# Block-sparse attention feeding a GELU MLP on one Trainium2 core: sampled value rows fetched by GpSimd row gathers from an SBUF list instead of block copies from registers

## The chip, the cores and the metric

One core of a Trainium2 chip runs the whole program: TensorE (PE; its weight loads are listed as PEld), VectorE (DVE), ScalarE (ACT), GpSimd (POOL) and SyncE (SP), each with its own in-order instruction queue, and 16 DMA engines that serve the DMAs which SP, POOL and ACT issue. The metric is the device time of one execution, in microseconds.

## The reference

Batch 4, 8 heads, 768 tokens, head size 64, all in float32. Tokens are in 24 blocks of 32. A query block sees itself and its neighbours, the first and the last block, and three sampled blocks; the first and the last query block see everything. The result goes, token by token, through a two-layer network.

```python
mask = np.abs(blk_i - blk_j) <= window            # window = 1
mask = mask | (blk_i == 0) | (blk_j == 0) | (blk_i == n_blocks - 1) | (blk_j == n_blocks - 1)
for qb in range(n_blocks):
    for kb in sampled_blocks[qb]:                 # 3 random blocks, int64
        mask[qb * block:(qb + 1) * block, kb * block:(kb + 1) * block] = True
scores = np.where(mask, scores, -1e9)             # scores = q k^T / 8, softmax, times v
...
x = attn_out.transpose(0, 2, 1, 3).reshape(B * S, H * D)     # 3072 x 512
h = x @ w_in                                      # 512 -> 2048
g = 0.5 * h * (1.0 + erf(h * inv_sqrt2))
return g @ w_out                                  # 2048 -> 512
```

A sampled block may repeat another one, or lie in the window or among the global blocks; it counts once.

## The kernel before

The work is cut into eight units, (batch b, half hf) for b = 0..3 and hf = 0, 1; a unit is 12 query blocks (384 tokens). For each unit the kernel runs attention and then the first layer (`ffn1_step`, 8 steps, PE then GELU on ACT); the second layer (`ffn2_pieces`) is fed as filler between the steps of the *next* unit's attention. The order on every engine is the order of the Python program (the schedule is manual), and the framework adds the semaphore waits.

A unit has 8 groups: two for its dense block (4 heads each) and six of one or two sparse blocks. For a sparse block all eight heads' scores stand in two rows of 256 columns: 96 of the window, 96 sampled, 32 + 32 of the two global blocks. `stage_scores` (L309) makes them on PE, DVE takes the maximum (L329), `stage_exp` (L347) the exponential on ACT, `stage_transpose` and `stage_evict` (L359, L367) turn the probabilities, `stage_av` (L388) multiplies them with the values, `stage_x` brings the result into `xT` for the first layer.

Gathered operands lie in SBUF. `kg` holds, for the 11 sparse blocks of a unit, the sampled keys (columns 0 to 95) and the global keys (96 to 159); it is filled by copies out of `kT` at an offset in a register (`k_sampled`, L251; `k_unit` shares them out between POOL and DVE) and by `k_globals` (L242). There is one `kg` for all units. The window's keys are read straight from `kT`. Values go a longer way: v is loaded (`load_v`: two halves of heads `vx` and the rows of the first and last block, `vgl`), copied on DVE or ACT into `vn` (`v_rows`, with columns of ones for the sum), written to a scratch in DRAM (`v_scratch`, `vscr`, one row of 528 numbers = 1056 bytes per token, and a 25th block of zeros), and read back as the operands `vg0s`, `vg1s` (one pair per half, 128 rows each): window rows by `v_window` (L282), sampled blocks by `v_sampled` (L265), one DMA of 32 rows (33 KB) for each of 11 x 3 sampled blocks of a unit, global rows by copies from `vgl` (`v_ends`, L272 to L277). A sampled block that repeats another or lies in the window reads the block of zeros instead; `value_list` (L173) works out these numbers once on DVE, 5 us of short operations on 72 numbers. Block numbers used as offsets are loaded into registers of the engine that issues (`block_numbers`, L205).

Row order in the value operands before: `vg0s` rows 0 to 95 window, 96 to 127 sampled 0; `vg1s` rows 0 to 63 sampled 1 and 2, 64 to 127 global. The columns of the scores are in the same order.

What sets the order around the change: POOL's queue carries all loads of inputs and weights (they cast to bf16), half of the key copies, the `v_ends` of the first halves, and 108 of the 264 sampled value DMAs; SP's queue carries the scratch writes, the window DMAs, 156 sampled value DMAs and the output stores. At the start POOL issues k, q, `vgl`, k, q, v; then `v_ends(0, 0)`, 18 key copies for blocks 6 to 11, then values mixed with the weight loads. PE starts with 36 transposes of the identity (L524) that nobody reads, then transposes k and q (`prep_pair`, L224). During the first layer of unit (0,0) the lists for the second half are loaded and `second_values` (L556) issues the second half's values and then the loads of batch 1. From unit 1 on, `steps` holds what is issued between the first layer's steps and `later` what is issued between the next attention's groups.

```python
def v_sampled(b, j, r):
    queue, val = (nc.gpsimd, v_pool[j, r]) if (j, r) in v_pool else (nc.sync, v_sp[j, r])
    hf, u = (j - 1) // US, (j - 1) % US
    dst = vg0s[hf][96:128, u, :] if r == 0 else vg1s[hf][BL * r - BL:BL * r, u, :]
    queue.dma_start(out=dst, in_=vscr[b][bass.ds(val * BL, BL), :])
```

## Time and profile before

| | |
|---|---|
| time, median of 3 runs | 350.5 us (350.29 to 351.52) |
| profiled execution | 350.54 us, of which the span, first to last instruction, is 348.6 |
| PE busy | 300.2 us (86%) |
| ACT busy | 221.3 us (63%) |
| DVE busy | 191.6 us (55%) |
| POOL busy | 134.4 us (39%) |
| DMA | 42.27 MB, 43807 packets |
| value DMAs of 33 KB | 156 on SP, 108 on POOL (0.537 us of POOL each, 57.5 in all) |
| key copies into `kg` | 106 on POOL (25.9 us), 158 on DVE (18.8 us) |

The page gives busy time by engine, then 40 slices of the span with the granted PE clock and the DMA share in tenths, then the chain of work that ended last, as shares by engine and line, then groups of equal instructions. Times in the order of time are us from the span's start; a bracket behind a line is the time that the engine stood idle before it, and what released it. "issue" there is idle time for which the profile shows no cause; "SPq" is time in SP's own queue.

### The profile page before, as it was taken

How to read it: one execution, taken by the hardware profiler on the slowest of the kernel's cores; microseconds unless marked ns; L12 is line 12 of the kernel's file. 1: busy time of each engine (PE TensorE's matmuls, PEld its weight loads, DVE VectorE, ACT ScalarE, POOL GpSimd, SP SyncE). 2: the span in 40 equal slices, each digit the busy share in tenths (PEclk: the TensorE clock that was granted, in tenths of full speed). 3: DMA queues.
4: the chain of work that ended last, by engine and by line, in shares of the span. 5: the costliest groups of instructions: out<-in, count | busy, mean ns of one | idle time of the engine just before them, and what ended most of it. 6: DMA issues, size and time to landing. Idle time of an engine off the chain costs nothing.

```text
span 348.6 us, 13273 instructions
## 1 busy us (share of the span) xinstructions
PE 300.2 (86%) x5284; PEld 168.5 (48%) x5284; DVE 191.6 (55%) x569; ACT 221.3 (63%) x370; POOL 134.4 (39%) x269
## 2 busy tenths in 40 slices
PE   6456789986998889977998989997998989998996
PEld 5233445443553445444454445444554545454575
DVE  7395543673774765266473766276473764276100
ACT  2364725785467776786557885697567876778540
POOL 7767609901488271777400410966101310000000
PEclk9655659999999999999999999999999999999999
DMA  7949999898388935898870313996440310000002
GB/s 102 148 148 193 198 198 166 162 235 190 125 192 141 211 91 187 183 174 142 161 167 0 73 49 125 200 184 145 109 104 2 81 40 32 0 35 34 30 22 72
DMA packets 43807, 42.27 MB, mean 121 GB/s; under 512 B 7969, under 2 KB 38690, under 8 KB 43746
## 3 DMA queue, kind: packets, MB, share of 16 engines
q0 software_dynamic: 22528, 17.55, 32.3%
q1 hardware_dynamic: 20786, 23.48, 24.5%
q8 instruction: 41, 0.67, 0.8%
q10 hardware_dynamic: 432, 0.39, 0.3%
q14 instruction: 20, 0.16, 0.1%
HBM read 45.63 MB, written 9.67 MB: 159 GB/s over the span
## 4 chain that ended last, share of the span: by engine, by line
PE 51%; ACT 20%; DMA 10%; issue 9%; DVE 4%; SPq 4%; POOL 1%; DVEq 0%; ACTq 0%; POOLq 0%
PE hp L429 21%; PE op L438 13%; ACT pp L347 10%; DMA vg<-vscr 6%; ACT ps L367 4%; PE tp L359 4%; PE av L388 4%; SPq L265 3%; PE op L459 3%; PE pt L224 3%; DMA vx<-in_v_dram 3%; PE sc L314 2%; ACT os L443 2%; ACT g L431 2%; ACT L431 1%
## 5 line engine op out<-in xcount | busy, mean ns | idle before, releaser
L438 PE MATMUL op<-w_out_sb,g 128*128 128x512 bf16 x336 | 95.0, 381 | 2.2 <-ACT os L443 1.6
L429 PE MATMUL hp<-xT,w_in_sb 128*128 128x384 bf16 x512 | 91.8, 332 | 0.9 <-ACT g L431 0.6
L265 POOL DMA_DIRECT2D vg<-vscr x108 | 57.5, 537 | 55.6 <-issue 23.0
L431 ACT ACTIVATE g<-hp 128x768 bf16<-128x768 f32 x64 | 51.7, 811 | 37.5 <-PE hp L429 37.4
L347 ACT ACTIVATE pp<-sc,nm 128x256 bf16<-128x256 f32 x176 | 69.0, 488 | 0.1
L329 DVE TENSOR_REDUCE nm<-sc 128x4 f32<-128x1024 f32 (+1 forms) x48 | 54.5, 1136 | 26.1 <-ACT ps L367 9.8
L367 ACT COPY ps<-tp 128x1024 bf16<-128x1024 bf16 (+1 forms) x48 | 45.2, 941 | 36.9 <-PE tp L359 36.9
L429 PEld LDWEIGHTS <-w_in_sb 128*128 128x128 bf16 x512 | 48.8, 99 | 36.4 <-issue 5.7
L251 POOL COPY kg<-kT 128x128 bf16 x106 | 25.9, 293 | 64.5 <-PE sc L314 56.1
L359 PE MATMUL tp<-identity,pp 128*128 128x128 bf16 x448 | 44.7, 230 | 6.7 <-ACT pp L350 3.2
L359 PEld LDWEIGHTS <-pp 128*128 128x128 bf16 x448 | 31.4, 107 | 29.0 <-ACT pp L347 9.0
L388 PE MATMUL av<-vg,ps 128*32 128x65 bf16 x1408 | 22.9, 200 | 20.2 <-ACT ps L367 9.2
L336 DVE TENSOR_REDUCE nm<-sc 128x1 f32<-128x768 f32 x16 | 15.3, 955 | 44.6 <-PE sc L314 44.6
L388 PEld LDWEIGHTS <-ps 128*32 128x32 bf16 x1792 | 19.5, 98 | 35.8 <-ACT ps L367 20.9
L438 PEld LDWEIGHTS <-g 128*128 128x128 bf16 x336 | 24.8, 98 | 20.9 <-issue 11.3
L314 PE MATMUL sc<-kT,qT 64*32 64x96 bf16 (+2 forms) x832 | 27.6, 236 | 3.5 <-ACT qT L236 2.8
L314 PEld LDWEIGHTS <-qT 64*32 64x32 bf16 x1536 | 14.1, 93 | 31.6 <-issue 26.1
L443 ACT COPY os<-op 128x512 f32<-128x512 f32 x21 | 12.4, 593 | 25.8 <-PE op L438 25.8
L401 DVE TENSOR_TENSOR xh<-av,rec 128x256 bf16<-128x256 f32 (+1 forms) x64 | 22.9, 358 | 2.2
L234 DVE COPY kT<-pt 128x768 bf16<-128x768 bf16 x14 | 13.4, 956 | 16.5 <-PE pt L224 16.4
L394 DVE TENSOR_SCALAR den<-av 128x4 f32<-128x4 f32 (+1 forms) x64 | 9.9, 155 | 20.1 <-PE av L388 20.1
L314 PE MATMUL sc<-kg,qT 64*32 64x160 bf16 x704 | 18.2, 240 | 2.0 <-issue 1.8
(67 smaller groups left out, 277.5 us busy)
## 6 DMA issues: line engine op xcount, KB each, us to landing
vg<-vscr SPq DMA_DIRECT2D x20, 297.0 KB, 5.2
out_dram<-os SPq DMA_DIRECT2D x21, 256.0 KB, 2.1
vg<-vscr SPq DMA_DIRECT2D x156, 33.0 KB, 4.4
vg<-vscr POOLq DMA_DIRECT2D x108, 33.0 KB, 4.1
kn<-in_k_dram POOLq DMA_DIRECT2D x8, 384.0 KB, 6.4
vx<-in_v_dram POOLq DMA_DIRECT2D x8, 384.0 KB, 9.5
vscr<-vn SPq DMA_DIRECT2D x3, 792.0 KB, 3.3
qn<-in_q_dram POOLq DMA_DIRECT2D x6, 384.0 KB, 7.8
```

What stands on the lines that cost most here:

```text
L251: copy(kg[:, (j - 1) % US, :, BL * r:BL + BL * r], kTs[b % 2][:, :, bass.ds(vals[j, r] * BL, BL)])
L265: queue.dma_start(out=dst, in_=vscr[b][bass.ds(val * BL, BL), :])
L314: nc.tensor.matmul(out_, lhsT=qT[rows, h // 2, j * BL:(j + 1) * BL], rhs=rhs[rows], start=True, stop=True)
L329: nc.vector.tensor_reduce(out=nm[:, 0:2 * n].rearrange("p (j g) -> p j g", g=2), in_=A4[:, 0:n], op=ALU.max, axis=AX.X, negate=True)
L347: nc.scalar.activation(pp[:, 256 * n:256 * n + 256], A[:, c:c + 256], AF.Exp, bias=nm[:, n:n + 1])
L359: nc.tensor.transpose(T[:, c, :], pp[:, cols], identity)
L367: nc.scalar.copy(ps[:, 0:n, :], T[:, 0:n, :])
L388: nc.tensor.matmul(av[32 * hh:32 * hh + 32, s, :], lhsT=probs[:, 32 * hh:32 * hh + 32], rhs=vals[:, VW * h:VW * h + D + 1], start=(c == 0) ...
L401: nc.vector.tensor_tensor(xh[:, at:at + n, :], av[:, 0:n, 0:D], rec[:, 0:n, None].to_broadcast([P, n, D]), op=ALU.mult)
L429: nc.tensor.matmul(hp[:, i, 0:UT], lhsT=w_in_sb[:, ki, (m + i) * P:(m + i + 1) * P], rhs=xT[:, ki, :], start=(ki == 0), stop=(ki == KIN - 1))
L431: nc.scalar.activation(g[:, m:m + 2, :], hp[:, :, 0:UT], AF.Gelu)
L438: nc.tensor.matmul(op, lhsT=g[:, m, t * P:(t + 1) * P], rhs=w_out_sb[:, m, :], start=(m == 0), stop=(m == KOUT - 1))
```

## The change

It replaces the block copies of sampled values by row gathers. A new tile `vrows` holds, for each of 96 rows (3 blocks of 32) and each of the 24 query blocks, the number of the scratch row to read. `value_rows` builds it: the list is cast to bf16, multiplied on PE with a row of ones so that it stands on 96 partitions (`seen`), and DVE makes 32 x block + row out of it, with `pcol`, three iotas of POOL. `v_sampled` is then one indirect DMA on POOL per query block, 96 rows of 1056 bytes: 88 in all. No value numbers are loaded into registers any more.

So that one gather has one destination, the rows change their order: `vg0s` rows 0 to 95 sampled, 96 to 127 the window's first block; `vg1s` rows 0 to 63 the window's other two, 64 to 127 global. The score columns follow, which splits the products of a sparse block from two per head (96, 160 columns) into three (96, 96, 64). A window is now two DMAs (`part`).

Further: `vgl` is loaded after both halves of v at the start; DVE's first key numbers are loaded before the value list; the key copies of blocks 6 to 11 of the later batches move from DVE to POOL (`k_unit`); `v_ends` of the later batches' first halves move from POOL to DVE; `second_values` comes at the beginning of the first layer of unit (0,0), ahead of the key copies for unit (0,1); loads of q and k of the next batch move from `later` to `steps`, windows and gathers of its first half to `later`, and v loads from `steps` to the end of `later`.

```diff
-    first_v = load_v(0)
-    first_v[2]()
     load_k(0, HALVES[1])
     load_q(0, HALVES[1], slice(0, 64))
-    for f in first_v[:2]:
+    for f in load_v(0):
         f()
+    pcol = const.tile([SW, 1], F32, name="pcol")
+    for r in range(NR):
+        nc.gpsimd.iota(pcol[BL * r:BL * r + BL], pattern=[[0, 1]], base=0, channel_multiplier=1,
+                       allow_small_or_imprecise_dtypes=True)
...
+    def value_rows():
+        vfb = const.tile([1, NB, NR], BF16, name="vfb")
+        nc.vector.tensor_copy(vfb, vf)
+        ones = const.tile([1, SW], BF16, name="ones")
+        nc.vector.memset(ones, 1.0)
+        seen = psV.tile([SW, NB, NR], F32, name="seen", tag="av")
+        nc.tensor.matmul(seen.rearrange("p j r -> p (j r)"), lhsT=ones,
+                         rhs=vfb.rearrange("p j r -> p (j r)"), start=True, stop=True)
+        for r in range(NR):
+            rows = slice(BL * r, BL * r + BL)
+            nc.vector.tensor_scalar(vrows[rows], seen[rows, :, r], float(BL), pcol[rows, 0:1],
+                                    op0=ALU.mult, op1=ALU.add)
...
-    def v_sampled(b, j, r):
-        queue, val = (nc.gpsimd, v_pool[j, r]) if (j, r) in v_pool else (nc.sync, v_sp[j, r])
+    def v_sampled(b, j):
         hf, u = (j - 1) // US, (j - 1) % US
-        dst = vg0s[hf][96:128, u, :] if r == 0 else vg1s[hf][BL * r - BL:BL * r, u, :]
-        queue.dma_start(out=dst, in_=vscr[b][bass.ds(val * BL, BL), :])
+        nc.gpsimd.indirect_dma_start(
+            out=vg0s[hf][0:SW, u, :], out_offset=None, in_=vscr[b][:, :],
+            in_offset=bass.IndirectOffsetOnAxis(ap=vrows[:, j:j + 1], axis=0))
...
+    def v_window(b, hf, a, z, part):
+        r0 = (US * hf + a + part) * BL
+        dst = vg1s[hf][0:2 * BL, a:z, :] if part else vg0s[hf][SW:P, a:z, :]
...
+        moved = [lambda a=a, z=z, part=part: v_window(b, hf, a, z, part)
+                 for a, z, part in ((0, US, 0), (0, 6, 1), (6, US, 1))]
+        return moved, [lambda j=j: v_sampled(b, j) for j in range(1 + US * hf, 1 + US * hf + US)]
...
-                for c0, c1 in ((0, 96), (96, 256)):
+                for c0, c1 in ((0, SW), (SW, 192), (192, 256)):
                     for hh in range(4):
...
+    k_dve = block_numbers(ids, J0[:5], RS, DVE)
     value_list()
-    lists = [numbers_list(vf, J0[:6], (0, 1), SP), numbers_list(vf, J0[6:], (0,), SP)]
-    v_pool = block_numbers(vf, J0[:6], (2,), POOL) | block_numbers(vf, J0[6:], (1, 2), POOL)
+    value_rows()
...
     def k_unit(hf, b, js):
-        if hf:
+        if (hf, b) != (0, 0):
             k_sampled(b, js, k_pool, nc.gpsimd.tensor_copy)
         k_sampled(b, js, k_dve, nc.vector.tensor_copy)
...
             if u == 0:
                 k_dve |= block_numbers(ids, J1, (2,), DVE)
-                k_pool = block_numbers(ids, J1, (0, 1), POOL)
-                v_pool |= block_numbers(vf, J1, (2,), POOL)
+                k_pool |= block_numbers(ids, J1, (0, 1), POOL)
+                second_values()
             if nxt and not fresh:
                 k_unit(1, b, J1)
...
-                v_ends(1, 0, nc.gpsimd.tensor_copy)
+                v_ends(1, 0, nc.vector.tensor_copy)
...
                 if fresh:
-                    steps, later = v_fetch(b + 1, 1)
+                    moved, rows = v_fetch(b + 1, 1)
+                    steps, later = moved + rows[:5], rows[5:]
                     if b + 2 < B:
-                        steps = steps + load_v(b + 2)
+                        later = later + load_v(b + 2)
                 elif nxt and b + 1 < B:
-                    steps, later = v_fetch(b + 1, 0)
                     v_rows(b + 1, nc.vector.tensor_copy)
...
+                    moved, later = v_fetch(b + 1, 0)
+                    steps = load_qk(b + 1)
+                    steps[0] = lambda f=steps[0]: (v_scratch(b + 1), f())
+                    later = moved + later
...
-                if u == 0 and s == 5:
-                    k_dve |= block_numbers(ids, J0[5:], RS, DVE)
-                    second_values()
```

## The prediction

> **What bounds the kernel now.** I read the page first (shares, slices, the chain that ended last), then busy time by stage, then the order of time on PE and on POOL.
>
> ```profile
> span 348.6 us, 13273 instructions
> PE 300.2 (86%) x5284; PEld 168.5 (48%) x5284; DVE 191.6 (55%) x569; ACT 221.3 (63%) x370; POOL 134.4 (39%) x269
> PEclk9655659999999999999999999999999999999999
> DMA  7949999898388935898870313996440310000002
> PE 51%; ACT 20%; DMA 10%; issue 9%; DVE 4%; SPq 4%; POOL 1%; DVEq 0%; ACTq 0%; POOLq 0%
> ```
>
> PE carries half of the chain; DMA, SP's queue and "issue" hold 23%, and it is there that the change works: the clock is low and the DMA engines full in the first 52 us. By stage (us of the stretch, then busy time of PE, PEld, DVE, ACT, POOL, the granted clock, DMA share, GB/s):
>
> ```profile
> 16.00:46.60 30.60, 19.68 (x486) 11.43 (x485) 21.43 (x61) 18.35 (x34) 18.76 (x43) 0.56 0.87 176
> 62.50:90.40 27.90, 22.91 (x527) 11.85 (x526) 17.36 (x42) 17.09 (x34) 11.01 (x13) 1.00 0.94 180
> 106.30:132.00 25.70, 22.14 (x529) 11.88 (x530) 16.32 (x43) 17.95 (x35) 14.55 (x40) 1.00 0.73 145
> 143.30:170.80 27.50, 22.20 (x529) 11.69 (x526) 16.45 (x41) 18.26 (x35) 19.08 (x29) 1.00 0.87 154
> 222.70:248.00 25.30, 22.13 (x529) 11.71 (x526) 16.18 (x41) 18.28 (x35) 16.97 (x29) 1.00 0.74 144
> 299.90:324.20 24.30, 22.16 (x529) 11.53 (x526) 16.35 (x41) 18.19 (x35) 0.00 (x0) 1.00 0.07 25
> ```
>
> These are attention stretches, units (0,0), (0,1), (1,0), (1,1), (2,1), (3,1). The last has no traffic and takes 24.3; that is the floor. Over it the others lose 3.6, 1.4, 3.2 and 1.0: 9.2 us is all that better fetching of values can give after the start. On PE and POOL:
>
> ```profile
> 2.99 4.02 PE L524 MATMUL idle<-identity 128*128 128x128 bf16 x36 [2.99 <-POOL identity masks.py:199]
> 13.21 0.85 PE L224 MATMUL pt<-identity,kn 128*64 128x128 bf16 x12 [4.30 <-DMA kn<-in_k_dram]
> 34.59 0.36 PE L388 MATMUL av<-vg,ps 128*32 128x65 bf16 x12 [0.80 <-DMA vg<-vscr]
> 80.73 0.19 PE L388 MATMUL av<-vg,ps 128*32 128x65 bf16 x1 [2.63 <-issue]
> ```
>
> ```profile
> 11.68 4.58 POOL L277 COPY vg<-vgl 64x5280 bf16<-64x5280 bf16 x1
> 16.53 4.38 POOL L251 COPY kg<-kT 128x128 bf16 x18 [0.26 <-ACT kT L232]
> 39.71 0.62 POOL L106 DMA_DIRECT2D qn<-in_q_dram  x1 [2.54 <-DMA w_in_sb<-in_moe_w_in_dram]
> 51.68 5.25 POOL L251 COPY kg<-kT 128x128 bf16 x22 [8.09 <-issue]
> 56.87 6.64 POOL L265 DMA_DIRECT2D vg<-vscr  x11
> 63.50 1.59 POOL L100 DMA_DIRECT2D kn<-in_k_dram  x2
> ```
>
> PE sits idle for keys until 13.21, for values until 34.59, and stands 2.63 before 80.73 behind values landing at 77.78 in the chain. POOL has the key copies of unit (0,1) done at 56.9, ahead of its 11 value DMAs and the eight loads of batch 1. The qn load waiting for w_in shows that POOL's DMAs take eight completion semaphores in turn: each waits until the one eight before it has landed.
>
> **Part by part.** The profiled execution took 350.54 us (span 348.6 and 1.94 around it), the median of the runs is 350.5; the sum is made against 350.54.
>
> *The row list at the start.* DVE now loads 15 block numbers into registers before the value list: a copy of 0.15 and a load whose rows lasted 1.30 to 1.79 (median 1.57), +1.7. The list, done at 8.49, is done at 10.2; a cast of 0.2 follows, and the product `seen`. In the built program it stands first on PE, ahead of the 36 warm-up transposes. These start at 10.6 instead of 2.99 and end at 14.6; the k and q transposes, 2.0 + 2.8 us in two bursts, follow at 14.6 instead of ending at 16.0. First scores come at 18 to 19 instead of 15.95. DVE copies v only behind its kT copies, so the scratch write (18.79) moves as far: +2.0 to +2.7.
>
> *Global rows last, on POOL.* The vgl loads go behind v, whose last half landed at 18.0; so vgl lands near 18 (the queue holds the same bytes). POOL's copy of them (0.62 + 4.58), at 11.0 before, runs 18.0 to 23.3, the 18 key copies (4.38) to 27.7. The scratch is readable at about 25.5, so POOL is 2 us late for the first gather.
>
> *The gather.* 264 DMAs of 33 KB (156 on SP at 0.32, 108 on POOL at 0.54) become 88 on POOL. No row shows one. Below: 0.50, the median of one 33 KB issue. Above: 1.61, three issues of 0.537 for the same 96 rows. Rows cost POOL little (w_in, 512 rows, 0.78; w_out, 1024 rows, 0.90) but reading 96 row numbers is new; I take the middle, 1.05, and keep both ends. The second gather is issued at 28.8 and lands 4.1 later (the POOL row), with 0.5 for the longer issue 33.4. Group 0's av, 28.26 before, then starts at 33.4 and ends at 34.3; group 1 follows at the undisturbed 3.1 and from group 1's end to ffn1 took 11.7 (34.95 to 46.67): 49.1. Gathers 5 to 8 queue behind w_in: +0.3. Start: **+2.7** (1.5 to 4.2).
>
> *Unit (0,1).* The second half's windows go out at once on SP, and its late values (3.6 lost) go. But in POOL's order the 11 gathers and the eight loads of batch 1 now stand before the 22 key copies. POOL's idx load ends at 53.4 (51.68, less one load of 1.3, plus 2.7, rounded up); gathers 1 to 6 to 59.7. The seventh and eighth take the semaphores of w_out: issued at 44 and 45 (41.8 and 42.7 plus 2), landed 12.8 to 17.0 later, with more traffic beside them, at 58 and 63.5. Gathers 8 to 11 end at 67.7, loads (1.59 + 1.51 + 1.53 + 1.24) at 73.6, the four copies that the first sparse scores need at 74.5. Those scores are due at 65.71 + 2.7 = 68.4; PE is in order, so it stops for 5.8 to 6.1. I take 5.8 lost in place of 3.6: **+2.2** (-2.5 to +6).
>
> *Later units.* Values of (1,0) no longer wait behind SP's queue: gathers from 100 to 112, first wanted at 122: -1.3. (1,1) and (2,1): the loads of q and k move ahead and some 20 small DMAs per unit leave SP (156 over 8); part of their losses is PE standing inside a group of matmuls ("issue" 1.87 and 1.41 with DMA full), which may stay: -1.8 of 3.2, -0.5 of 1.0. Together **-3.6** (-5.6 to 0).
>
> *Column order.* 88 sparse blocks get 8 more weight loads and products each: 704. Eight products of 160 columns start every 67 ns, eight of 96 every 50; 96+96+64 with at least 50 each makes +30 ns per block, 2.6 us in all, of which part falls where PE waits for exp (2.1 us idle per undisturbed unit): **+1.3** (0 to 2.6).
>
> *At nothing.* 54 key copies go from DVE (0.104 each) to POOL (0.24): 4.3 us per batch in a stretch where POOL was busy 2.4 of 16.4; what uses them, group 2, is scored 9 us after the unit starts; uncovered, they cost 4.3 a batch. Three v_ends go from POOL (5.2) to DVE (1.8) in ffn1 of (b,0), where DVE was busy 4 of 11; uncovered, they hold the next dense maximum, 1.8 each. DVE's v copy, 2.82 beside POOL's 4.59 copy at 89.3 against 1.58 else, may gain 1.2 that no one waits for. Three iotas (0.46) lie in POOL's wait for vgl.
>
> Sum: 2.7 + 2.2 - 3.6 + 1.3 = +2.6, so 353.1.
>
> *A row against it.* One POOL issue of a value DMA took 2.96 instead of 0.50, at 96.2, beside DVE's copies of kT and kg (95.95 to 100.4); 1 of 16 in that stretch. The Trainium skill ("SBUF — State Buffer", section "SBUF: two separate sides", the box on the "DVE blocks DMA" trap) says that GpSimd cannot write its descriptors while VectorE runs a copy in a two-port mode, and that DMAs of SP are immune. By this page, 156 DMAs leave the immune queue, and the sum is the third rival's. The row agrees in its direction; in which mode DVE copied, no row tells.
>
> **Rivals.**
> 1. *Cheap gather, faster.* At 0.54 a gather, the second lands at 32.3 (start +1.6), gathers 8 to 11 end at 62, the copies at 68.8 against 67.3 due: 1.5 lost in place of 3.6, -2.1. With -3.6 and +0.8: -3.3, **347.2**. It decides below about 0.8 us a gather (from -3.3 at 0.54 to +2.6 at 1.05). For it: POOL's packets are cheap. Against: three such issues are what the same rows cost now.
> 2. *Dear gather.* At 1.61: start +4.2; gathers of (0,1) end at 72.6, copies at 79.4 against 69.9, 9.5 lost, +5.9; batch 2's v load, behind 22 gathers and 18 copies, lands near 155 and DVE, in order, holds (1,1)'s first maximum for some 5: later units +3.2; +1.3. **365**.
> 3. *POOL starved by DVE copies.* 1 of 16 gathers at +2.0: of the 22 of batch 0 that lie on the path 2.7 us, **355.8**. Against it: during (0,0) DVE mostly reads PSUM.
> 4. *No change that counts:* the copies of (0,1) come in time (w_out lands by 60) and the start costs 1.5 more only: 1.5 + 0.8 + 1.3 - 3.6 = 0, **350.5**.
>
> **How the numbers follow.** No change can be told within 0.5% (1.75 us). Forecast 0.45 (own range 351.5 to 357), cheap gather 0.28, dear gather 0.09, starving 0.08, no change 0.10. The forecast lies in "same" for a tenth of its chance: same 0.14; faster 0.28 with 0.02 of the no-change case, 0.30; slower 0.56. The range takes in the cheap gather's sum and reaches toward the dear one: 346.5 to 362.
>
> **What would show it.** After: `seen` before the warm-up, which starts near 10.6; first scores at 18 to 19; the gather's POOL duration (0.8 decides); ffn1 of (0,0) starting near 49.4; a PE gap of some 6 us before (0,1)'s first sparse scores near 68, ended by POOL's key copies; (1,0) to (2,1) near 24.5. Wrong would be: key copies of (0,1) done before 68, or a PE that no longer stands in (1,1), which would bring the full 5.6.

## The result, and the profile after

The changed kernel takes 430.5 us (median of 4 runs, 429.2 to 433.5) against 351.0 us of the kernel before on the same chip (350.3 to 356.3): a ratio of 1.2285, 95% interval 1.220 to 1.237. The run of 356.3 us was in a slower state of the chip and is not in the ratio. It is 23% slower; the forecast of 353.1 us and its range were passed by far. From the page of the changed kernel (span, busy time, granted clock and DMA share in 40 slices, the chain that ended last):

```profile
span 428.6 us, 13889 instructions
PE 316.9 (74%) x5933; PEld 185.3 (43%) x5989; DVE 194.8 (45%) x519; ACT 222.1 (52%) x370; POOL 158.2 (37%) x300
PEclk9955559889995969995999969995999979999999
DMA  8559993590395372962133372952124310000102
PE 48%; ACT 16%; issue 13%; another core or an unknown queue 10%; DVE 7%; DMA 3%; POOL 2%; DVEq 1%; SPq 0%; ACTq 0%; POOLq 0%
```

No engine has become the bound: all are idler than before, POOL at 37% too. What has grown in the chain is "issue" (9% before, 13% now) and releases from an "unknown queue" (10%, before none), and the granted clock falls every few slices. By stage, the attention of (0,0), (0,1), (1,0), (1,1) and (3,1), and last one stretch of gathers (columns as in the prediction's table):

```profile
17.50:62.20 44.70, 20.69 (x580) 13.87 (x575) 24.47 (x62) 18.60 (x34) 24.74 (x38) 0.54 0.93 182
77.20:112.08 34.88, 26.54 (x626) 14.06 (x633) 17.99 (x44) 19.54 (x36) 13.80 (x33) 0.90 0.59 99
139.00:173.40 34.40, 26.32 (x626) 14.83 (x633) 15.97 (x42) 19.68 (x36) 18.69 (x38) 0.88 0.49 88
184.20:220.40 36.20, 24.75 (x613) 14.10 (x621) 16.03 (x41) 18.76 (x35) 9.88 (x11) 0.86 0.29 72
377.30:404.10 26.80, 22.02 (x613) 12.59 (x621) 16.25 (x41) 18.67 (x35) 0.00 (x0) 1.00 0.07 23
233.56:245.54 11.98, 7.52 (x71) 3.01 (x71) 1.18 (x3) 5.07 (x7) 9.23 (x10) 1.00 0.28 76
```

Behind the start, the attention stretches with gathers shown here have lost 7.6 to 9.4 us against (3,1), which has none; and it is not the DMA engines: their share in (1,1) is 0.29, in the stretch of ten gathers 0.28. PE had 71 matmuls in those 12 us; an undisturbed attention has 613 in 26.8. PE and POOL in one such stretch, in the order of time:

```profile
122.79 0.53 PE L243 MATMUL pt<-identity,qn 128*64 128x128 bf16 x12
123.55 0.32 PE L444 MATMUL hp<-xT,w_in_sb 128*128 128x384 bf16 x1 [0.24 <-issue]
124.96 0.32 PE L444 MATMUL hp<-xT,w_in_sb 128*128 128x384 bf16 x1 [1.09 <-issue]
125.70 0.32 PE L444 MATMUL hp<-xT,w_in_sb 128*128 128x384 bf16 x1 [0.41 <-issue]
127.14 0.48 PE L444 MATMUL hp<-xT,w_in_sb 128*128 128x384 bf16 x1 [1.12 <-issue]
128.57 0.49 PE L444 MATMUL hp<-xT,w_in_sb 128*128 128x384 bf16 x1 [0.95 <-issue]
130.69 0.48 PE L444 MATMUL hp<-xT,w_in_sb 128*128 128x384 bf16 x1 [1.63 <-issue]
```

```profile
125.23 0.91 POOL L282 DMA_INDIRECT vg<-vscr,vrows  x1 [0.30 <-issue]
126.45 0.91 POOL L282 DMA_INDIRECT vg<-vscr,vrows  x1 [0.30 <-issue]
127.66 0.92 POOL L282 DMA_INDIRECT vg<-vscr,vrows  x1 [0.31 <-issue]
```

The six single matmuls are of one step of the first layer and wait for nothing that the profile shows; from one to the next it takes one, two or three times 0.71 us. `w_in` landed long before. A gather takes 0.92 us of POOL and 0.30 between two. PE's waits in total, longest last (us, times, longest):

```profile
PE sc L328 <- issue: 34.3, 39, 1.9
PE op L453 <- issue: 9.1, 49, 0.3
PE hp L444 <- issue: 8.7, 8, 1.6
PE av L403 <- issue: 6.0, 10, 1.3
```

The second of these lines is no loss. In this profile 56 of the 336 second-layer products of L453 have no record (the page counts 280 here and 336 in e15), and these short waits of 0.16 or 0.33 us are put down where one is missing: profiles with all 336 have none of them. Of the 62 us of "issue" in all, 53 are left without that line; of e1's 24, 17.

The start went nearly as the prediction had it:

```profile
10.66 0.29 PE L205 MATMUL seen<-vfb,ones 1*96 1x72 bf16 x1 [10.66 <-DVE ones L203]
10.88 3.70 PE L538 MATMUL idle<-identity 128*128 128x128 bf16 x36
17.55 0.43 PE L328 MATMUL sc<-kT,qT 64*32 64x512 bf16 x3
18.60 0.53 PE L328 MATMUL sc<-kT,qT 64*32 64x512 bf16 x13 [0.62 <-ACT qT L255]
```

The start of each unit's first layer (us; its first `hp` matmul in the order of time) shows where time is lost, here and in some of the experiments:

| kernel | (0,0) | (0,1) | (1,0) | (1,1) | (2,0) | (2,1) | (3,0) | (3,1) |
|---|---|---|---|---|---|---|---|---|
| before | 46.67 | 90.27 | 132.02 | 170.69 | 211.44 | 247.87 | 288.62 | 324.08 |
| changed | 62.20 | 112.08 | 173.47 | 220.44 | 270.03 | 317.10 | 366.57 | 404.17 |
| e1, plain DMAs for gathers | 51.95 | 98.46 | 142.63 | 178.59 | 221.31 | 258.29 | 299.61 | 336.88 |
| e3, before with three products | 46.18 | 93.03 | 138.99 | 177.74 | 218.55 | 255.70 | 296.75 | 332.25 |
| e8, before with the new start | 50.52 | 95.97 | 137.73 | 175.79 | 216.53 | 253.11 | 293.84 | 329.29 |
| e9, every second a plain DMA | 53.50 | 102.47 | 143.54 | 181.25 | 225.32 | 261.76 | 302.84 | 340.12 |
| e12, a small DMA behind each gather | 56.71 | 118.31 | 164.47 | 213.18 | 259.41 | 300.84 | 346.15 | 383.54 |
| e13, a copy behind each gather | 55.47 | 110.54 | 159.24 | 203.46 | 251.67 | 294.18 | 339.00 | 375.69 |
| e14, a plain DMA behind each pair | 55.62 | 104.30 | 156.67 | 198.25 | 244.88 | 287.44 | 330.99 | 367.22 |
| e15, gathers among key copies | 54.70 | 99.43 | 142.04 | 182.74 | 223.80 | 259.44 | 300.73 | 338.10 |
| e16, spaced and joined | 56.74 | 95.86 | 137.33 | 173.88 | 214.62 | 250.07 | 290.80 | 326.25 |

### The profile page after: what moved, and what is told of

Read it like the earlier page. It is cut to its first block, busy times and chain, and to the rows that moved or that the text cites. A ratio compares the mean times of both kernels' runs of the same rounds, so it can differ in the third digit from the quotient of the medians.

```text
span 428.6 us, 13889 instructions
## 1 busy us (share of the span) xinstructions
PE 316.9 (74%) x5933; PEld 185.3 (43%) x5989; DVE 194.8 (45%) x519; ACT 222.1 (52%) x370; POOL 158.2 (37%) x300
## 3 DMA queue, kind: packets, MB, share of 16 engines
q1 hardware_dynamic: 13250, 18.20, 15.7%
## 4 chain that ended last, share of the span: by engine, by line
PE 48%; ACT 16%; issue 13%; another core or an unknown queue 10%; DVE 7%; DMA 3%; POOL 2%; DVEq 1%; SPq 0%; ACTq 0%; POOLq 0%
PE hp L444 16%; PE op L453 11%; ACT pp L362 6%; PE sc L328 4%; PE tp L374 4%; PE av L403 4%; ACT ps L382 3%; PE pt L243 3%; PE op L474 2%; DVE nm L344 2%; DMA vg<-vscr,vrows 2%; POOL vg L282 2%; ACT os L458 1%; ACT g L446 1%
## 5 line engine op out<-in xcount | busy, mean ns | idle before, releaser
L282 POOL DMA_INDIRECT vg<-vscr,vrows x88 | 82.5, 938 | 115.5 <-issue 52.9
L444 PE MATMUL hp<-xT,w_in_sb 128*128 128x384 bf16 x512 | 94.0, 334 | 10.3 <-issue 8.7
L453 PE MATMUL op<-w_out_sb,g 128*128 128x512 bf16 x280 | 88.0, 401 | 10.6 <-issue 9.1
L270 POOL COPY kg<-kT 128x128 bf16 x160 | 39.8, 299 | 77.8 <-DVE kT L253 44.0
L328 PEld LDWEIGHTS <-qT 64*32 64x32 bf16 x2240 | 25.6, 95 | 78.0 <-issue 67.0
L374 PE MATMUL tp<-identity,pp 128*128 128x128 bf16 x448 | 46.3, 240 | 9.3 <-ACT pp L365 6.5
L328 PE MATMUL sc<-kT,qT 64*32 64x96 bf16 (+2 forms) x832 | 36.6, 240 | 20.7 <-issue 14.1
L328 PE MATMUL sc<-kg,qT 64*32 64x96 bf16 (+1 forms) x1408 | 31.6, 213 | 25.9 <-issue 20.1
L374 PEld LDWEIGHTS <-pp 128*128 128x128 bf16 x448 | 34.3, 111 | 32.1 <-ACT pp L365 9.1
L453 PEld LDWEIGHTS <-g 128*128 128x128 bf16 x336 | 25.5, 100 | 18.7 <-issue 9.2
L255 ACT ACTIVATE qT<-pt 128x768 bf16<-128x768 bf16 (+1 forms) x16 | 11.6, 732 | 25.9 <-PE pt L243 13.9
```

What stands on the lines that cost most here:

```text
L270: copy(kg[:, (j - 1) % US, :, BL * r:BL + BL * r], kTs[b % 2][:, :, bass.ds(vals[j, r] * BL, BL)])
L282: nc.gpsimd.indirect_dma_start(out=vg0s[hf][0:SW, u, :], out_offset=None, in_=vscr[b][:, :], in_offset=bass.IndirectOffsetOnAxis(ap=vrows[ ...
L328: nc.tensor.matmul(out_, lhsT=qT[rows, h // 2, j * BL:(j + 1) * BL], rhs=rhs[rows], start=True, stop=True)
L374: nc.tensor.transpose(T[:, c, :], pp[:, cols], identity)
L444: nc.tensor.matmul(hp[:, i, 0:UT], lhsT=w_in_sb[:, ki, (m + i) * P:(m + i + 1) * P], rhs=xT[:, ki, :], start=(ki == 0), stop=(ki == KIN - 1))
L453: nc.tensor.matmul(op, lhsT=g[:, m, t * P:(t + 1) * P], rhs=w_out_sb[:, m, :], start=(m == 0), stop=(m == KOUT - 1))
```

## Experiments: is it the gather?

**e1, plain DMAs in the gathers' place.** Three explanations stood: runs of gathers (G), the three-way cut with its 704 more products (S), POOL's order and the start (O).

```diff
-        nc.gpsimd.indirect_dma_start(
-            out=vg0s[hf][0:SW, u, :], out_offset=None, in_=vscr[b][:, :],
-            in_offset=bass.IndirectOffsetOnAxis(ap=vrows[:, j:j + 1], axis=0))
+        nc.gpsimd.dma_start(out=vg0s[hf][0:SW, u, :],
+                            in_=vscr[b][(j - 1) * BL:(j + 2) * BL, :])
```

> The gather is replaced by a plain DMA of the same size on the same queue (96 rows of 1056 bytes, blocks j-1 to j+1 instead of the sampled ones, so the sampled values are wrong); everything else stays. Theory G (runs of indirect gathers make TensorE stand inside its groups): the seven stretches in which TensorE trickles disappear, 66 to 80 us of the 80 come back, 346 to 360 us. Rival S (the three-way column split, 704 more weight loads and products, is what TensorE cannot keep up with): the split stays, 410 us or more. Rival O (POOL's order: key copies behind the value fetches, the later start): the order stays and only POOL's time falls from 1.2 to about 0.5 us a fetch, 395 us or more.

363.3 us (ratio 1.0354, 1.032 to 1.039): 67 of the 80 us come back, and the time is 3 us above G's band; S and O fall as the main cause. The group of fetches and PE's largest "issue" wait after it:

```profile
L282 POOL DMA_DIRECT2D vg<-vscr x88 | 44.9, 520 | 90.9 <-DMA vscr<-vn 49.9 <-PE av L402 9.7 <-DVE kg L270 8.3
PE sc L327 <- issue: 8.7, 7, 2.0
```

**e2, 11 more gathers near the end.**

```diff
+        if (b, hf) == (B - 1, 1):
+            for j in J0:
+                v_sampled(B - 1, j)
         attention(b, hf, ...)
```

> The changed kernel, with 11 more gathers at the start of unit (3,1)'s attention, into a buffer that nobody reads any more. There nothing else moves: no loads, no key copies on POOL. Theory G: TensorE trickles there as well, from 5 to 9 us after the first of them to some 2.5 us after the last, and the run is 5 to 12 us longer, 435 to 443 us. Rivals S and O, and a rival that the gathers only hurt beside other transfers: the unit stays at 26.3 us and the run at 429 to 434 us.

446.1 us in one run, 15.7 over the changed kernel and 3 above G's band. The gathers ran earlier than meant, from 363.7 on, as soon as (3,0) had read the buffer's slots, and (3,0) lost most of it: its first layer starts at 381.8 instead of 366.6, and 2.5 of these 15 us had gone before that unit. There are no loads there and still an engine stands, DVE:

```profile
373.42 0.92 POOL L282 DMA_INDIRECT vg<-vscr,vrows  x1 [0.31 <-issue]
375.36 0.91 POOL L282 DMA_INDIRECT vg<-vscr,vrows  x1 [1.02 <-remote]
376.55 0.16 DVE L409 TENSOR_SCALAR den<-av 128x4 f32<-128x4 f32 x1 [11.42 <-remote]
378.57 0.41 PE L403 MATMUL av<-vg,ps 128*32 128x65 bf16 x16 [11.05 <-DVE ps L384]
```

The `av` that `den` reads ended at 366.2. DVE, with nothing else to do, starts ten us later, behind the tenth of the eleven gathers, and PE waits for what DVE does next.

**e5 and e6, fewer rows and shorter rows.**

```diff
-            out=vg0s[hf][0:SW, u, :], ... ap=vrows[:, j:j + 1]
+            out=vg0s[hf][0:BL, u, :], ... ap=vrows[0:BL, j:j + 1]        # e5
+            out=vg0s[hf][0:SW, u, 0:132], in_=vscr[b] as rows of 132 ... # e6
```

> The changed kernel, each of its 88 gathers cut to the first 32 of its 96 rows; the other 64 rows of a block come unsampled with the window transfer of SyncE, so two of three sampled value blocks are wrong. With the plain DMA of the first experiment in its place the gather's cost is 430 - 363 = 67 us. If that goes by rows (or by bytes), a third of it stays: 385 us (375 to 395). If it goes by the number of gathers: 425 to 435 us.

> The changed kernel, each gather still of 96 rows, but of the first 264 bytes of a row instead of 1056; the other columns come unsampled with the window transfer of SyncE, so the sampled values of six of eight heads are wrong. If the 67 us go by rows or by the number of gathers: 425 to 435 us. If they go by bytes, a quarter stays: 380 us (372 to 390).

431.2 and 429.8 us. Neither rows nor bytes count; the number of gathers seems to. POOL's time for one hardly changes either (890 and 939 ns, against 938).

## Experiments: what came with the gather

**e3, the cut in three alone.**

```diff
-                for c0, c1 in ((0, 96), (96, 256)):
+                for c0, c1 in ((0, 96), (96, 192), (192, 256)):
```

> The kernel before, with only its sparse score products cut in three (columns 0 to 96, 96 to 192, 192 to 256) instead of two: 704 more weight loads and products, nothing else. Theory G: what the prediction put down for it, 0 to 2.6 us, so 350.5 to 353.5 us. Rival S: 400 us or more. Rival O: as G.

361.0 us (four runs, 358.7, twice 361.0, and 366.0), ratio 1.0335 (1.026 to 1.041). That ratio has the run of 366.0 in it; the other three have a mean of 360.2, 9.3 us over the kernel before. So it is some 10 us, neither theory's number. The profiled execution shows where: PE stands inside groups, longest in (0,1) and (1,0).

```profile
82.29 0.22 PE L314 MATMUL sc<-kg,qT 64*32 64x64 bf16 x8 [3.58 <-issue]
123.66 0.21 PE L388 MATMUL av<-vg,ps 128*32 128x65 bf16 x2 [3.82 <-issue]
165.10 0.30 PE L388 MATMUL av<-vg,ps 128*32 128x65 bf16 x16 [2.17 <-issue]
243.00 0.24 PE L314 MATMUL sc<-kT,qT 64*32 64x96 bf16 x8 [1.24 <-issue]
q8 instruction: 47, 0.77, 0.9%
```

The last line is the queue that brings instructions: 47 packets of 16,384 bytes. The kernel before has 41, its five stops of that sort 6.9 us together. The packets' own records tie the two together: the blocks landed at 80.89, 122.11, 163.62 and 241.67, and the stops above end 1.40, 1.55, 1.48 and 1.33 us later. In the kernel before, the stops that end at 80.73, 161.48 and 238.72 do so 1.46, 1.41 and 1.38 us after a landing; of the two small ones, 0.39 and 0.56 us, the second ends 1.84 after. The first of these is the stop of 2.63 us that the prediction put down to values landing at 77.78. That is theory I: PE waits for its next block of instructions. The 5933 matmuls and 5989 weight loads recorded in the changed kernel, in 47 blocks, make 254 a block. The Trainium skill ("Runtime: NRT & Kernel Launch", section "Instruction fetch mechanics") says that instructions come in blocks of 256 over a DMA queue of the engine, which the traces agree with, and that crossing into a new block is mostly hidden. Here it is not hidden in the densest stretches of attention, where in this run the fetches of two blocks begin as little as 3.4 to 4 us apart. These "issue" waits, without those for missing records, sum to 12.8 us here and 7.1 before; the rest of the 10 us no run divides up.

**e8, the new start alone.** The global rows last, the register load ahead of the list, the list's product ahead of the warm-up.

```diff
-    first_v = load_v(0)
-    first_v[2]()
     load_k(0, HALVES[1]); load_q(0, HALVES[1], slice(0, 64))
-    for f in first_v[:2]:
+    for f in load_v(0):
         f()
...
+    k_dve = block_numbers(ids, J0[:5], RS, DVE)
     value_list()
+    value_rows()
```

> The kernel before, with only the changed start: the register load of the key numbers ahead of the value list on VectorE, the list's product ahead of TensorE's 36 warm-up transposes (its result is not used), the global rows of v loaded last. The prediction's terms for it, without the gather's own: first scores at 18 to 19, fetches 2 us later, ffn1 of (0,0) at 48 to 49 instead of 46.7, 352 to 354 us. Rival (the start is hidden behind what comes later in (0,0)): 350 to 351 us. If the start were what costs the changed kernel its time: 400 us or more.

355.8 us, ratio 1.0106 (1.002 to 1.019). The first layer of (0,0) starts 3.9 later, that of (0,1) 5.7; the order of PE's work at the start is that of the changed kernel. The prediction's term was 2.7.

**e10, e1 with the key copies of (0,1) ahead of the fetches again.**

```diff
+                k_unit(1, b, J1)
                 second_values()
-            if nxt and not fresh:
+            elif nxt and not fresh:
                 k_unit(1, b, J1)
```

> The first experiment (plain DMAs in the gathers' place, sampled values wrong), with POOL's 22 key copies of unit (0,1) put back ahead of the value fetches and the eight loads of batch 1. The prediction's step for unit (0,1): the copies came late, so its attention (32.1 us there, 29.5 in the kernel before) falls to about 29.5, and the run to 360 to 361.5 us. Theory I (that unit's loss comes from late instruction blocks, since the cut in three stays): 32 us and 362.5 to 364 us.

360.7 us (1.0283, 1.022 to 1.035) against 363.3 (1.032 to 1.039, so the intervals overlap), and the attention of (0,1) in the profiled execution takes 29.7 instead of 32.1: the prediction's step holds, at the price of a plain DMA.

## Experiments: when does a gather hold the others?

**e4, one gather per group.** Each gather of five units waits behind a one-element copy of the newest row maximum.

```diff
+            nc.gpsimd.tensor_copy(gate, st["nm"][0:1, 0:1])
             v_sampled(...)
```

> The changed kernel, but from the fetch for unit (1,1) on (five runs of 11 gathers) each gather waits behind a one-element POOL copy of the row maximum of one more group of scores, so that they are issued one per group, about 2.3 us apart, instead of 1.22. Theory G in the form that it is the density of the run that counts: these five stretches lose under 3 us each instead of 8 to 11, so 385 to 410 us. G in the form that every gather costs TensorE its share: 425 to 432 us. Rivals S and O: 425 to 432 us.

436.9 us (1.245): no gain from distance. So far, then, a price per gather. The trace says more. Two stops around one gather, and the end of a unit:

```profile
302.40 0.94 POOL L282 DMA_INDIRECT vg<-vscr,vrows  x1 [0.50 <-issue]
302.99 0.22 PE L328 MATMUL sc<-kg,qT 64*32 64x64 bf16 x2 [0.36 <-issue]
303.73 0.51 PE L403 MATMUL av<-vg,ps 128*32 128x65 bf16 x31 [0.39 <-issue]
317.32 0.16 DVE L409 TENSOR_SCALAR den<-av 128x4 f32<-128x4 f32 x1 [4.27 <-remote]
```

The gate opened each gather just as PE went into its densest stretch (80 matmuls and 80 weight loads of scores and `av`); PE stands, but for three matmuls, until 0.4 us after the gather's end. The next two gathers, at 306.18 and 309.93, have such a stop of 0.5 us as well, each ending 1.3 us after the gather's start. And the last three gates were open already, so that four gathers ended the unit in a row, beside DVE's 4.27. So where PE is densest one gather alone, 3 us or more from the next, stops it.

**e9, every second gather a plain DMA.**

```diff
+        if j % 2:
+            nc.gpsimd.dma_start(out=vg0s[hf][0:SW, u, :], in_=vscr[b][(j - 1) * BL:(j + 2) * BL, :])
+            return
```

> The changed kernel with half of its gathers (44, those of even blocks) and the plain DMA of the first experiment for the odd blocks, whose sampled values are wrong. If every gather costs the other engines the same, 67/88 = 0.76 us each: 363 + 44 x 0.76 = 397 us (390 to 405). If it is the runs that cost, whatever their length: 415 us or more; if only long runs cost (the trickle began after several gathers): 370 to 380 us.

365.4 us (1.041, 1.035 to 1.047): below all three bands. 44 gathers, 1.8 us or more from start to start and five or six to a unit, cost next to nothing; a fixed price per gather has fallen.

**e12, e13, e14.** Does the plain DMA behind a gather help, or the time it takes?

```diff
         nc.gpsimd.indirect_dma_start(...)
+        nc.gpsimd.dma_start(out=tiny[0:1, j, :], in_=vscr[b][S:S + 1, 0:64])   # e12
+        nc.gpsimd.tensor_copy(dull, zrow)                                      # e13
...
+        if j % 3 == 0:   # e14: a plain DMA instead, as in e9
```

> The changed kernel, all 88 gathers, and behind each of them one plain DMA of 128 bytes on the same queue (its data is not used). With half of the gathers replaced by plain DMAs the cost was not 33 us but nothing (365.4 against 363.3), although gathers one group apart had cost as much as gathers back to back. Theory D (what holds the other engines lasts from a gather to the next plain DMA of POOL): 363 to 375 us, with POOL busier by some 0.6 us a block. Rival N (a cost by number that sets in between 44 and 88 gathers): 430 us or more.

> The changed kernel with a POOL copy of 32 x 528 elements (0.6 us, its result is not used) behind each gather instead of the small DMA. Theory D: a copy ends nothing, 430 us or more. Rival T (POOL's time away from gathers is what counts, 0.85 us between two of them in the half-and-half kernel): 363 to 375 us. Rival N: 430 us or more.

> The changed kernel with plain DMAs for every third block (28 of 88; their sampled values are wrong), so that gathers come in pairs with a plain DMA behind each pair. Theory D with a cost for each gather that has no plain DMA behind it: about 30 of them, 363 + 30 x 0.76 = 386 us. If one gather's effect is only felt after more than two in a row: 363 to 368 us. Rival N: by number, 60 gathers, between 365 and 430, about 390 us.

409.8 us (1.163), 401.1 (1.141) and 392.8 (1.118): D's and T's numbers are missed alike, and so are N's in e12 and e13; e14 is 3 us above N's "about 390" and 7 above D's 386. PE's waits in e12 are of another kind:

```profile
PE sc L330 <- POOL kg L271: 19.2, 2, 17.7
PE tp L376 <- ACT pp L367: 10.7, 3, 6.3
PE sc L330 <- issue: 8.8, 19, 1.0
```

"issue" before the scores is back at the level of e1 (8.8 against 34.3), while PE waits 19.2 us for key copies, because POOL spends 1.8 us instead of 1.2 on a block's fetch and does the copies behind it. In all, "issue" (without the waits for missing records) is 16 us in e12 and 22 in e13 and e14, against e1's 17 and the changed kernel's 53.

That is only part of it. 17.7 of the 19.2 us are one wait, in (0,1). From the first layer of (1,0) to that of (3,0) PE never waits for POOL's key copies, and by the table this stretch takes 157 us in e1 and 159 in e9, but 174 in e14, 180 in e13, 182 in e12 and 193 in the changed kernel. The gathers of e12 and e13 stand 1.79 and 1.75 us from start to start, as those of e9, with ten to twelve in a run where e9 has five or six; and in both there are still stops like those of e4, as here in e13:

```profile
230.46 0.95 POOL L283 DMA_INDIRECT vg<-vscr,vrows  x1 [0.17 <-PE av L405]
231.83 0.28 PE L330 MATMUL sc<-kg,qT 64*32 64x96 bf16 x5 [0.51 <-issue]
```

PE goes on 0.42 us after the gather's end. An "issue" stop of more than 0.2 us that ends 0.30 to 0.55 us after a gather's end follows 26 of the 88 gathers in e4, 19 in e13, 12 in e12 and none in e9. So distance took away the longest stops, not the cost.

**e15, the gathers among the key copies.** Work between the gathers that POOL has to do anyway:

```diff
-            k_sampled(b, js, k_pool, nc.gpsimd.tensor_copy)
+            for j in js:
+                v_sampled(b, j)
+                k_sampled(b, [j], k_pool, nc.gpsimd.tensor_copy)
```

> The changed kernel, all 88 gathers, but no two of them in a row: each gather of a unit stands directly ahead of the one or two POOL key copies of the same block (0.24 us each), which POOL has to do anyway; in unit (0,0) one key copy follows each gather. Theory T (the other engines run dry during a gather and recover as soon as POOL leaves 0.5 us or more between two, so only runs cost): issue waits of TensorE fall from 62 us to the 24 of the first experiment, and the run to 357 to 366 us, POOL not being late. Rival N (every gather costs 0.4 to 0.76 us wherever it stands): 395 us or more.

362.4 us (1.0319, 1.028 to 1.035), with all 88 gathers: as fast as e1, which has none. PE's waits before the scores, and the gathers' group, whose time has not changed:

```profile
PE sc L328 <- issue: 8.4, 5, 3.6
L282 POOL DMA_INDIRECT vg<-vscr,vrows x88 | 82.5, 938 | 49.4 <-issue 33.9 <-DMA vscr<-vn 11.3 <-DMA vx<-in_v_dram 2.1
```

So the 67 us go with the arrangement of the gathers and not with their number or their time on POOL, and N falls. In all, "issue" is 10.8 us here against e1's 17. What is left of it are fetches: the stops of 3.57 and 3.13 us, the longest, end 1.44 and 1.28 us behind a landing, and no gather has a stop of e4's kind behind it. Other than the expectation says, blocks 1 to 5 of the later first halves have no POOL copies; five gathers in a row, then, are cheap enough. e15 also has e10's order for (0,1); against e10's 360.7 it is 1.7 us longer, within the intervals.

T's number is met, but its reason is not shown. Half of the gathers stand 1.4 to 1.7 us from start to start here, closer than in e12 and e13, and in (2,0) eleven of them run through the densest part of attention without a stop. What the key copies do that e13's copy and e12's DMA don't, no run shows; e15 moved the gathers and spaced them in one step.

**e17, eight in a row where PE needs little.** In the changed kernel PE ran on for 99 to 146 matmuls and weight loads after the first gather of a run, until its first "issue" wait of over 0.3 us (in seven of eight runs 120 or more).

```diff
                 ffn1_step(2 * s)
+                if (b, hf, s) == (B - 1, 1, 0):
+                    nc.gpsimd.tensor_copy(gate, g[0:1, 0, 0:1])
+                    for j in J0[:8]:
+                        v_sampled(B - 1, j)
```

> The spaced version, and eight gathers in a row more (into a buffer that nobody reads any more), released by the first gelu of the last unit's feed-forward, where TensorE needs only 112 instructions for the remaining 9 us. In the changed kernel TensorE went on for 93 to 144 instructions, mostly 117 to 134, after the first gather of a run before it stood. Theory C (it is the supply of instructions that stops, and some 130 are in hand): this feed-forward stays at 10.7 to 11.2 us. Rival H (signals between the engines are held too, whatever the number of instructions): its gelus and products come 4 us or more later, 14.7 us or more.

364.9 us in one run, and the feed-forward takes 10.71 us as ever:

```profile
341.50 7.96 PE L444 MATMUL hp<-xT,w_in_sb 128*128 128x384 bf16 x48 [0.15 <-ACT g L446]
341.84 0.94 POOL L282 DMA_INDIRECT vg<-vscr,vrows  x1
343.00 0.81 ACT L446 ACTIVATE g<-hp 128x768 bf16<-128x768 f32 x1 [0.80 <-PE hp L444]
348.20 0.81 ACT L446 ACTIVATE g<-hp 128x768 bf16<-128x768 f32 x1 [0.49 <-PE hp L444]
350.39 0.91 POOL L282 DMA_INDIRECT vg<-vscr,vrows  x1 [0.30 <-issue]
```

Eight gathers back to back, and PE and ACT pass their work on in their usual 1.30 us. This speaks for C, that a run stops the supply of PE's instructions and some 130 are in hand, and against H for the signals between PE and ACT. C is not the whole of it: e4's single gathers stop PE after far fewer instructions (10, 19 and 49 behind the three gathers named there), and e2's DVE stood for ten us with its operand ready.

## Experiments: fewer products

**e7, one product per sparse block; e11, earlier fetches for (0,1) besides.** If blocks of instructions are late, fewer instructions must help.

```diff
-                for c0, c1 in ((0, 96), (96, 256)):
+                for c0, c1 in ((0, 96), (96, 256)) if (b, hf) == (0, 0) else ((0, 256),):
...
+    def k_window(hf, b, copy):        # window keys into kg, columns 0 to 95
+        for c in range(3):
+            s0 = (US * hf + c) * BL
+            copy(kg[:, :, :, BL * c:BL * c + BL],
+                 kTs[b % 2][:, :, s0:s0 + US * BL].rearrange("p h (j c) -> p j h c", c=BL))
...
-                if u == 0 and s == 5:                                      # e11
+                if u == 0 and s == 0:
                     second_values()
```

> The kernel before, with the keys of the window copied beside the sampled ones (three copies of 128 x 11 x 4 x 32 per unit, on VectorE for the second halves, on GpSimd for the first ones), so that a sparse block's scores are one product of 256 columns instead of two of 96 and 160; unit (0,0) keeps two. 616 products and weight loads fewer. Theory I (TensorE stands inside groups because the block of its next 256 instructions lands late, and the cut in three cost 8 to 10 us by such stops): the five stops of the kernel before, 6.9 us, shrink or go, and 8 x 10 ns a block come on top, 340 to 347 us. The prediction's reading (those stops come from full DMA engines and late values and stay): 348 to 352 us. If the copies get in VectorE's way: 352 us or more.

> The joined products, and besides the value fetches of unit (0,1) started after the first step of unit (0,0)'s feed-forward instead of the sixth, as the change did with its gathers. The joined kernel's (0,1) still waits some 2.4 us (0.71, 0.38 and 1.29 in three places, the last one for values). If the early start brings the values in time: 345.5 to 347 us. If the DMA engines are full there anyway, or w_in and w_out come later for it: 347.5 to 350 us.

e7: 347.9 us, ratio 0.988 (0.978 to 0.998), 37 blocks, at the border of theory I's band and the other reading's; in its profiled execution no stop of PE over 0.35 us is put to "issue" (6.9 us before); one of 2.5 us that ends at 230.78, 1.59 behind a landing, is put to ACT. So the stops went, as I says, and the gain is smaller than I's band. e11: 345.5 us, 0.9857 (0.981 to 0.990), as by the first of its bands. Both beat the kernel before, by less than 2%.

**e16, e15's gathers with one product; e19, the same with the old start.** e16 joins e15 and e7. e19 besides fetches (0,0) by 33 plain DMAs from registers and makes the row list after that unit:

```diff
-            v_sampled(0, j)
+            for r in RS:
+                queue, val = (nc.gpsimd, v_pool[j, r]) if (j, r) in v_pool else (nc.sync, v_sp[j, r])
+                queue.dma_start(out=vg0s[0][BL * r:BL * r + BL, j - 1, :],
+                                in_=vscr[0][bass.ds(val * BL, BL), :])
```

> The same with the window's keys copied into the list (three VectorE copies per unit, 2.5 us) and one product of 256 columns per sparse block outside unit (0,0), 1232 products and weight loads fewer. Theory T with theory I (late instruction blocks): the cut in three cost about 10 us, the cut in two some 4, so 343 to 352 us. Rival N: 380 us or more.

> Spaced gathers and joined products for all units but (0,0); that unit is fetched by 33 plain DMAs with registers, as in the kernel before, with the start of the kernel before (global rows early, the list's product after (0,0) instead of ahead of the warm-up). In the spaced and joined run ffn1 of (0,0) began at 56.7, in the kernel before at 46.7, and all later units of the former sum to 294.0 us against 301.9. If the two halves add up: 340 to 344 us. If fetches of (0,1) collide with a start that ends earlier: 344 to 349 us.

e16: 350.8 us, 0.9993 (0.997 to 1.002), as fast as before: it loses 10.1 us until the first layer of (0,0) and is ahead of the kernel before by 7.9 from there to the last one's start. e19: 345.8 us (four runs, 342.5 to 347.7), 0.9813 (0.975 to 0.988). The two halves of e16 added up to 341; the runs lie in both bands, so whether a collision takes back part of the sum stays open. The best of this study are e11 and e19, equal within their intervals; one has gathers and one has none.

## Why the prediction was wrong

The sum held that a gather costs POOL's time and that what waits for POOL pays. **The step that failed is the gather**: "I take the middle, 1.05" was near (0.92 + 0.30 = 1.22, within 0.50 to 1.61), but every term and rival priced POOL alone. The 88 gathers, as the change arranged them, cost 67 us (e1), and not by POOL's time: with the same 0.94 us for each of them e15 is as fast as e1. PE and DVE stood where the profile shows nothing to wait for. No row of before has a gather, so none has such a stop, and the cost lay outside both bounds because both were POOL's.

- *Start, +2.7.* Right in kind: `seen` at 10.66, warm-up at 10.88, the first scores at 17.55 (18 to 19 expected, 15.95 before). e8 measured 4 us (0.8 to 6.7 by its interval); (0,1), with later loads, adds 1.9 that the step had not. In the changed kernel ffn1 of (0,0) came at 62.2 instead of 49.1; with plain DMAs it came at 52.0, so ten of these 13 us are the gathers.
- *Unit (0,1), +2.2.* The stop by key copies did not show, because PE was late for other reasons; with plain DMAs it is worth 2.4 (e10). Right in kind.
- *Later units, -3.6.* The losses were there to be had: with one product the attention of (1,1) and (2,1) takes 25.9 and 24.7 (e16), 28.0 and 25.7 before. But the largest of them were not fetches of values. The "issue" stops of 1.87 and 1.41 us, which the prediction noted "with DMA full", ended 1.41 and 1.38 us after an instruction block had landed, and the change adds six blocks.
- *Column order, +1.3 (0 to 2.6).* Mis-sized: some 10 us (e3; 9 to 14 by the interval, 9.3 without its longest run). The step counted what 704 products and weight loads take on PE, not that they have to be fetched.
- *At nothing.* Held: the key copies moved to POOL and `v_ends` moved to DVE leave e16's later units at the floor of 24.7 and 26.4.
- *Rivals.* None had the gather's effect on other engines, so none came near 430. "Dear gather" priced it at 1.61 where 1.22 was measured, and was 65 us short. "POOL starved" fell: one of 88 gathers took 1.92 us, the others 1.02 or less. That one, from 72.68 on, ended 0.12 us after DVE's copy of the global rows (72.96 to 74.48), which agrees in direction with what the Trainium skill weighed there says ("SBUF — State Buffer", section "SBUF: two separate sides"); ten others had a DVE copy beside them and were not longer, so it moves 1 us of the 80. The direction, slower, was right by the prediction's own steps for the start, the order and the columns only; that the gathers cost in the same direction was luck.

How it adds up: 67 by the gathers; of the 12.4 left, the cut costs about 10, the start 4 and POOL's order 2.7, each measured by itself. That is some 4 too much, and no run shows where they come back.

Open is what in a run of gathers stops the other engines, and why e15's arrangement does not while e12's and e13's still do. It isn't a late block: in the stretch shown above PE stood from 123.5 on, and the fetch of its next block began at 142.5, over 100 instructions later. It isn't DMA load: PE stood likewise in the stretch from 233.56 on, at a DMA share of 0.28, where each gather's packets were in 2.3 us after its issue, the first like the tenth. Whether DVE's late starts (e2, e4) have the same cause was not tried. All times were taken with the recording of instructions on, and what the runs cost without it no run shows.

## What to carry to other kernels

An operation has a price on its own engine and may have another on all the others: measure a new kind of operation once in the place where the others are busiest, and once in a row, before a kernel is built on it. In this kernel indirect gathers back to back cost 67 us in all, and the same gathers each ahead of key copies that were due anyway cost nothing that the runs can tell. Distance by itself was not enough: a copy or a small DMA put between them brought back less than half. So time the arrangement, and don't go by a spacing. Count TensorE's instructions as well as its time: a stop inside a group that waits for no semaphore and ends about 1.4 us after an instruction block has landed is a fetch, and fewer, larger products shortened it here.

## What the runs showed that was not expected

- Back-to-back indirect gathers (1.22 us apart) let PE go on for 99 to 146 matmuls and weight loads and then give it a few at ticks of 0.71 us. The effect is the same for 32 rows and 96, for 264 bytes and 1056. It is gone for five or six to a unit at 1.8 us from start to start (e9), among key copies at 1.4 to 1.9 (e15), and where fewer instructions are needed during the run (e17); it is not gone for ten to twelve in a run at 1.75 and 1.79 (e13, e12), nor for single gathers beside PE's densest work (e4).
- Instruction blocks of 256 cost up to 3.9 us a stop in attention, the stops of over 1 us outside runs of gathers ending 1.2 to 1.6 us after the landing; 704 more pairs of small instructions cost some 10 us, 616 fewer gained 3.8 (0.8 to 7.6 by the interval).
